# A fused sliding-window conv and ELU feed-forward layer: conv taps as the stationary operand, and one transposing transfer per super step

## The chip, the cores and the metric

The kernel runs on one core of one Trainium2 chip. The metric is the device time of one execution in microseconds (us), lower is better. Quoted times are medians of several runs. Scatter of the runs of one kernel: 0.2 to 0.4% from the lowest to the highest. The profile of an execution gives, for every instruction, its engine, start and length.

Engines are named as in the profile: PE is TensorE, PEld its weight loads, DVE is VectorE, ACT is ScalarE, POOL is GpSimd, SP is SyncE.

## The reference, cut to what matters

```python
# x: 8 x 4096 x 192 float32, weight: 8 heads x 7 taps
w = softmax(weight, axis=-1)
# causal window of 7 tokens, per head of 24 channels
out = einsum('hk,bskhg->bshg', w, windows_of(x_padded))     # "conv", 32768 tokens x 192
h = out @ w_in                                               # 192 -> 2048
g = where(h > 0, h, exp(min(h, 0)) - 1)                      # ELU
return g @ w_out                                             # 2048 -> 192, float32
```

## The kernel before

The 32768 tokens are worked off in 32 super steps of 1024 tokens (super step 0 is computed in another way at the start). A super step has 16 *pairs*. One pair is one block of 128 of the 2048 hidden columns for both halves of 512 tokens: three concurrent matmul pairs of the first product into one PSUM slot `H`, two EXPs on ACT, two clamps on POOL, and two DVE instructions that write `gT` and free the slot. PSUM is the memory that the matmuls write to. The kernel uses eight banks of it: `H` is three slots of two banks, `ops` takes two more as the accumulator of the second product. The conv of a coming super step has no bank of its own, so it takes an `H` slot too.

```python
# PE, first product of pair n: the slot must be free
k = slot_of_pair[n]
wait_slot(k)            # DVE is done with the pair that had it, or ACT with the conv
for j in range(3):
    for r in range(2):  # two row tiles, concurrent
        ins = pe.matmul(H[:, k % 3, GS * r : GS * (r + 1)],
                        w_in[HP * r : HP * (r + 1), j, FC * q : FC * (q + 1)],
                        att[HP * r : HP * (r + 1), s % 2, j, :], ...,
                        tile_position=(HP * r, 0))
# ... second product: "rounds" of two concurrent 64 x 128 x 192 matmuls from gT and w_out,
#     dealt out between the pairs; 64 rounds fill `ops` for one half (512 tokens)

# PE, conv half m: x is stationary (24 columns), the band of taps Tr is moving
for hb in range(2):
    for (w, c0, nc_, o) in PIECES[g]:
        for q in range(4):
            h = 4 * hb + q
            ins = pe.matmul(to[SLOT * q : SLOT * q + CPH, hb, o : o + nc_],
                            xg[:, s % NXB, w, CPH * h : CPH * (h + 1)],
                            Tr[:, h, CW - c0 - nc_ : CW - c0][:, ::-1],
                            start=True, stop=True, tile_position=(0, SLOT * q))

# ACT: clears the conv's slot into csb (1024 elements), and `ops` into osb once per half
a.activation(csb[:, m % 4, b0:b1, :], conv_bank(m)[:, b0:b1, :], ACT.Copy)
a.activation(osb[:, b, :, :, :].rearrange("p g k d -> p g (k d)"), ops[:, :, 0 : 2 * D], ACT.Copy)

# SP: csb goes to DRAM (`bounce`) and comes back in the layout that the first product needs
sy.dma_start(bounce[...], csb[:, m % 4, :, :])
for j in range(3):
    eng.dma_start(att[HP * g : HP * (g + 1), s % 2, j, :], src)

# DVE, pair n: ELU, and frees the slot
v.scalar_tensor_tensor(out=gT[:, s % NG3, q, u, :], in0=E[:, n % NE, u, :], scalar=1.0,
                       in1=H[:, slot_of_pair[n] % 3, GS * u : GS * (u + 1)],
                       op0=ALU.subtract, op1=ALU.max)
# ... (the start, the loads and the tail are cut)
```

## Time and profile before

| | before |
|---|---|
| time | 748.92 us (median of 4, 747.99 to 749.63) |
| span of the profiled run | 746.2 us |
| first osb evacuation | 39.01 us |
| mean half super step (8 pairs), pairs 64 to 447 | 11.341 us |

The page of the kernel before. The first line is the busy time of each engine; then come two lines of the chain that ended last (share of the span by engine, then by engine, tile and line); then groups of instructions: line, engine, operation, tiles, shapes, count, then busy us and mean ns of one, then idle time of the engine just before them.

```profile
PE 735.6 (99%) x13850; PEld 517.2 (69%) x13850; DVE 637.9 (85%) x1041; ACT 647.0 (87%) x1165; POOL 660.8 (89%) x1107
...
PE 96%; DVE 1%; ACT 1%; DMA 1%; issue 0%; POOL 0%; SPq 0%
PE ops L741 46%; PE H L706 45%; PE H L679 5%; DVE gT L561 1%; PE H L741 1%; DMA xf<-in_x_dram 1%; ACT E L499 0%; POOL E L410 0%; PE H L648 0%; PE ops L648 0%; ACT csb L479 0%; ACT xT L438 0%; PE H L616 0%; DVE xh L536 0%; SPq L755 0%
...
L561 DVE SCALAR_TENSOR_TENSOR gT<-E,H 128x512 f16<-128x512 f32 x1024 | 632.8, 682 | 92.8 <-POOL E L410 86.4
...
L741 PE MATMUL ops<-w_out,gT 64*128 64x192 f16 x8064 | 416.8, 243 | 0.3
L706 PE MATMUL H<-att,w_in 64*128 64x512 bf16 x3072 | 407.7, 377 | 2.5 <-DVE gT L561 1.9
...
L679 PE MATMUL H<-Tr,xg 128*24 128x122 bf16 (+1 forms) x2360 | 38.6, 209 | 0.0
```

PE is busy 99% and is 96% of the chain. A first-product matmul is recorded as 377 ns and a round's as 243 ns, but the next pair of matmuls starts 216 and 83 ns after the last. The records overlap by some 160 ns, so a gap of PE of up to 0.16 us doesn't show as idle time. To see it one has to subtract starts. The Trainium skill warns of this share in "Perfetto Trace Analysis", Identifying the Most-Contended Engine: matmul busy share is not a good measure of TensorE's distance from its limit. The busy share of the weight loads, one of the two measures that it names instead, is 69% here.

The timeline of PE around one conv of the kernel before (start us, length us, engine, line, operation, tiles, shapes, count):

```profile
589.14 0.82 PE L706 MATMUL H<-att,w_in 64*128 64x512 bf16 x6
589.80 0.99 PE L741 MATMUL ops<-w_out,gT 64*128 64x192 f16 x20
590.63 0.81 PE L706 MATMUL H<-att,w_in 64*128 64x512 bf16 x6
591.27 0.58 PE L741 MATMUL ops<-w_out,gT 64*128 64x192 f16 x10
591.78 0.65 PE L679 MATMUL H<-Tr,xg 128*24 128x122 bf16 x40
592.36 0.67 PE L741 MATMUL ops<-w_out,gT 64*128 64x192 f16 x12
592.87 0.81 PE L706 MATMUL H<-att,w_in 64*128 64x512 bf16 x6
```

Ten matmuls are five rounds: 591.27 + 5 x 0.083 = 591.68, but the conv (L679) starts at 591.78. That 0.10 us I take for the drain when the tiling mode changes. The conv then takes 0.58 us until the next round at 592.36. This 0.58 us holds a second drain, on the way back: in this half the last four conv matmuls, of 24 columns, start by 592.25, four such take 0.03 us, and the next round still starts only at 592.36. Over pairs 64 to 447 the way back costs 0.107 us in one half and 0.089 in the other.

From the starts of all matmuls between pairs 64 and 447 I added up what lies between them beyond the pitch of back-to-back work (0.2156 us a first-product pair of matmuls, 0.0827 us a round, 0.59 us a conv half). Before, a super step of 22.68 us has 0.20 us of drains ahead of conv and 0.33 us of gaps ahead of first products.

### The profile page before, as it was taken

Reading aid. Unit: us, or ns where it says so; the run is one execution under the profiler, and the core shown is the slowest. Engines: PE = TensorE matmul, PEld = TensorE weight load, DVE = VectorE, ACT = ScalarE, POOL = GpSimd, SP = SyncE. Lnnn points to the kernel's source line nnn. Section 1 sums busy time; section 2 is a strip of 40 time slices with the busy share of each in tenths; the row PEclk is TensorE's granted clock in tenths of the full one; section 3 lists DMA queues with packets and bytes.
Section 4 is the critical chain, followed back from the end, with each engine's and each line's share of the span. In section 5 each row is a group of like instructions: output and inputs, shape, how many; then the busy total and the mean of one; then the engine's idle time right before and its main releaser. Section 6 shows DMA issues by size and latency. Waiting matters only on the chain.

```text
span 746.2 us, 32212 instructions
## 1 busy us (share of the span) xinstructions
PE 735.6 (99%) x13850; PEld 517.2 (69%) x13850; DVE 637.9 (85%) x1041; ACT 647.0 (87%) x1165; POOL 660.8 (89%) x1107
## 2 busy tenths in 40 slices
PE   7899999999999999999999999999999999999998
PEld 4567777777777677776677777776776776777666
DVE  5988988888889889889889888888898898888894
ACT  6888888898888898888888888988888888888884
POOL 8888989989989989889989899899898898899883
PEclk9999999999999999999999999999999999999999
DMA  9654453453543543444434435535435435345112
GB/s 174 134 107 89 101 107 84 104 106 79 112 90 88 113 97 88 93 101 101 107 88 103 98 90 107 107 73 118 85 92 110 94 93 115 77 103 106 60 44 65
DMA packets 107038, 72.79 MB, mean 98 GB/s; under 512 B 44552, under 2 KB 106640, under 8 KB 106896
## 3 DMA queue, kind: packets, MB, share of 16 engines
q1 hardware_dynamic: 66384, 54.47, 24.0%
q0 software_dynamic: 40224, 15.78, 19.7%
q8 instruction: 108, 1.77, 1.0%
q10 hardware_dynamic: 288, 0.49, 0.2%
q14 instruction: 34, 0.28, 0.1%
HBM read 44.78 MB, written 41.42 MB: 116 GB/s over the span
## 4 chain that ended last, share of the span: by engine, by line
PE 96%; DVE 1%; ACT 1%; DMA 1%; issue 0%; POOL 0%; SPq 0%
PE ops L741 46%; PE H L706 45%; PE H L679 5%; DVE gT L561 1%; PE H L741 1%; DMA xf<-in_x_dram 1%; ACT E L499 0%; POOL E L410 0%; PE H L648 0%; PE ops L648 0%; ACT csb L479 0%; ACT xT L438 0%; PE H L616 0%; DVE xh L536 0%; SPq L755 0%
## 5 line engine op out<-in xcount | busy, mean ns | idle before, releaser
L561 DVE SCALAR_TENSOR_TENSOR gT<-E,H 128x512 f16<-128x512 f32 x1024 | 632.8, 682 | 92.8 <-POOL E L410 86.4
L410 POOL TENSOR_SCALAR E<-E 128x512 f32<-128x512 f32 x1024 | 604.3, 615 | 72.9 <-ACT E L499 68.0
L499 ACT ACTIVATE E<-H 128x512 f32<-128x512 f32 x1024 | 546.0, 605 | 83.3 <-PE H L706 74.6
L741 PEld LDWEIGHTS ops<-w_out,gT 64*128 64x128 f16 x8064 | 345.3, 94 | 106.6 <-ACT osb L470 10.8
L741 PE MATMUL ops<-w_out,gT 64*128 64x192 f16 x8064 | 416.8, 243 | 0.3
L706 PE MATMUL H<-att,w_in 64*128 64x512 bf16 x3072 | 407.7, 377 | 2.5 <-DVE gT L561 1.9
L706 PEld LDWEIGHTS H<-att,w_in 64*128 64x128 bf16 x3072 | 134.1, 94 | 99.2 <-issue 5.8
L479 ACT ACTIVATE csb<-H 128x1024 bf16<-128x1024 f32 x59 | 60.4, 1024 | 0.0
L470 ACT ACTIVATE osb<-ops 128x768 f32<-128x768 f32 x63 | 51.5, 817 | 6.2 <-PE ops L741 6.2
L362 POOL DMA_DIRECT2D xg<-in_x_dram x62 | 52.2, 842 | 0.4 <-issue 0.4
L679 PE MATMUL H<-Tr,xg 128*24 128x122 bf16 (+1 forms) x2360 | 38.6, 209 | 0.0
L679 PEld LDWEIGHTS H<-Tr,xg 128*24 128x24 bf16 x2360 | 29.6, 92 | 9.3 <-issue 9.3
L741 PE MATMUL H<-w_out,gT 64*128 64x192 f16 x128 | 5.9, 243 | 0.0
L572 DVE COPY osb<-H 128x192 f32<-128x192 f32 x1 | 0.4, 358 | 6.3 <-PE H L741 6.3
L741 PEld LDWEIGHTS H<-w_out,gT 64*128 64x128 f16 x128 | 5.3, 94 | 0.0
L592 PE MATMUL ops<-zw 128*128 128x512 bf16 x9 | 4.0, 631 | 1.2 <-DVE zw L511 1.2
L367 POOL DMA_DIRECT2D w_in<-in_moe_w_in_dram x7 | 4.6, 657 | 0.3 <-DMA wh<-in_weight_dram 0.3
L479 ACT ACTIVATE csb<-ops 128x512 bf16<-128x512 f32 x6 | 3.7, 623 | 0.3 <-PE ops L679 0.3
L597 PE MATMUL ops<-zw 64*128 64x512 bf16 x12 | 2.3, 380 | 1.7 <-ACT csb L479 1.7
L592 PEld LDWEIGHTS ops<-zw 128*128 128x128 bf16 x9 | 1.2, 142 | 3.2 <-issue 1.9
L679 PEld LDWEIGHTS ops<-Tr,xg 128*24 128x24 bf16 x120 | 1.6, 92 | 2.0 <-issue 2.0
L597 PEld LDWEIGHTS ops<-zw 64*128 64x128 bf16 x12 | 0.6, 94 | 3.1 <-ACT csb L479 2.7
(47 smaller groups left out, 26.1 us busy)
## 6 DMA issues: line engine op xcount, KB each, us to landing
out_dram<-osb SPq DMA_DIRECT2D x126, 192.0 KB, 2.7
conv_slots<-csb SPq DMA_DIRECT2D x62, 256.0 KB, 2.5
att<-conv_slots SPq DMA_DIRECT2D x186, 64.0 KB
xg<-in_x_dram POOLq DMA_DIRECT2D x31, 240.0 KB, 5.2
xg<-in_x_dram POOLq DMA_DIRECT2D x31, 192.0 KB, 4.5
w_out<-in_moe_w_out_dram POOLq DMA_DIRECT2D x1, 768.0 KB, 14.8
w_in<-in_moe_w_in_dram POOLq DMA_DIRECT2D x2, 240.0 KB, 8.0
xf<-in_x_dram ACTq DMA_DIRECT2D x1, 384.0 KB, 3.3
```

Source lines behind the costliest of these rows:

```text
L362: g.dma_start(xg[:, b, w0:w1, :], src).then_inc(s_x[b][part - 1], 16)
L367: g.dma_start(w_in[HP * r : HP * (r + 1), :, c0:c1], moe_w_in.rearrange("(p j) f -> p j f", j=3)[:, :, c0:c1],).then_inc(s_w[k], 16)
L410: g.tensor_scalar(out=E[:, n % NE, u, :], in0=E[:, n % NE, u, :], scalar1=1.0, scalar2=0.0, op0=ALU.min, op1=ALU.max,).then_inc(s_clp)
L470: a.activation(osb[:, b, :, :, :].rearrange("p g k d -> p g (k d)"), ops[:, :, 0 : 2 * D], ACT.Copy,).then_inc(s_oev)
L479: return a.activation(csb[:, m % 4, b0:b1, :], conv_bank(m)[:, b0:b1, :], ACT.Copy)
L499: a.activation(E[:, n % NE, u, :], H[:, k, GS * u : GS * (u + 1)], ACT.Exp).then_inc(s_exp)
L561: v.scalar_tensor_tensor(out=gT[:, s % NG3, q, u, :], in0=E[:, n % NE, u, :], scalar=1.0, in1=H[:, slot_of_pair[n] % 3, GS * u : GS * (u + ...
L592: pe.matmul(ops[:, 0, :], zw[:, 0:P], zw[:], start=True, stop=True)
L597: pe.matmul(ops[:, r, :], zw[HP * r : HP * (r + 1), 0:P], zw[HP * r : HP * (r + 1), :], start=True, stop=True, tile_position=(HP * r, 0),)
L679: ins = pe.matmul(to[SLOT * q : SLOT * q + CPH, hb, o : o + nc_], xg[:, s % NXB, w, CPH * h : CPH * (h + 1)], Tr[:, h, CW - c0 - nc_ : CW ...
L706: ins = pe.matmul(H[:, k % 3, GS * r : GS * (r + 1)], w_in[HP * r : HP * (r + 1), j, FC * q : FC * (q + 1)], att[HP * r : HP * (r + 1), s ...
L741: ins = pe.matmul(acc[:, g, d0 : d0 + D], gT[HP * rt : HP * (rt + 1), t % NG3, q, g, t0 : t0 + P], w_out[HP * rt : HP * (rt + 1), q, :], s ...
```

## The change

The intent: conv in the same tiling mode as both products, with no drain and fewer columns to stream; output already per token, so that one transposing transfer per super step replaces two writes to DRAM and six reads; a simpler load of the band. Since every conv half now takes four heads of *all* 1024 tokens, it needs both parts of x: the second part is needed half a super step sooner, and is loaded a whole one sooner. The third of the three early convs, at the start of the kernel, moves from after pair 10 to after pair 9. The core of the diff, with cuts marked by `...`:

```diff
+CW = 128
+TOK = 112
+WPG = 5
+HB = 2
+BN = HB * CPH * 2 * WPG        # 480
+GAP_SPLIT = 4
-EARLY_CONV = {3: (1, 0), 6: (1, 1), 10: (2, 0)}
+EARLY_CONV = {3: (1, 0), 6: (1, 1), 9: (2, 0)}
...
-        order.append(("c", m))
+        order.append(("c", m, 0))
+        between = []
+        if gap:
+            between, gap[:] = gap[:GAP_SPLIT], gap[GAP_SPLIT:]
+        if between:
+            order.append(("o", between))
+        order.append(("c", m, 1))
...
+        def turn_att(eng, s):
+            eng.dma_start_transpose(
+                out=att[:, s % 2, :, :].rearrange("p j (w t) -> p (j w) t", t=TOK),
+                in_=csb[0:TOK, s % 2, :],
+            ).then_inc(s_att[s % 2], 16)
...
+                    csb[:, s % 2, :].rearrange(
+                        "p (j v h i) -> p h j v i", j=3, v=2 * WPG, h=HEADS
+                    )[:, h0 : h0 + HB],
+                    conv_bank(m)[:, b, 0:BN].rearrange(
+                        "p (h v i j) -> p h j v i", h=HB, v=2 * WPG, j=3
+                    ),
...
+            v.tensor_copy(Tm[:], Tr[:, :, ::-1]).then_inc(s_tm)
...
-                    for part in range(g + 1):
-                        W(s_x[s % NXB][part], x_need[s, part])
+                        for part in range(2):
+                            W(s_x[s % NXB][part], x_need[s, part])
...
+                    for hh in range(HB):
+                        for rt in range(2):
+                            b = rt ^ turned
+                            h = 4 * u + HB * b + hh
+                            n1 = BN // HB
+                            ins = pe.matmul(
+                                to[:, b, n1 * hh : n1 * (hh + 1)],
+                                Tm[HP * rt : HP * (rt + 1), h, :],
+                                xg[HP * rt : HP * (rt + 1), s % NXB, :, :].rearrange(
+                                    "p (g w) d -> p w g d", g=2
+                                )[:, :, :, CPH * h : CPH * (h + 1)],
+                                start=(hh == 0 and not turned),
+                                stop=(hh == HB - 1 and turned == 1),
+                                tile_position=(HP * rt, 0),
+                            )
+                            if hh == HB - 1 and not turned:
+                                ins.then_inc(s_cs)
...
```

The kernel keeps the two row tiles from writing one bank at the same time, and each bank needs both, hence the two phases (`turned`), with four rounds between them.

More of the change, by code (lines that the diff above doesn't have):

```diff
@@ L19 @@
 CPH = 24
-SLOT = 32
-CW = 122
-ZW = 256
+CW = 128
[4 more added lines that the diff above has]
+GAP_SPLIT = 4
+TAP = 6
 GS = 512
@@ L25 @@
 PAD = KSIZE - 1
-NWIN = 9
 NXB = 2
@@ L41 @@
 HALO = 2
-XW = 5
-X_AT = ((3, 1), (8, 0), (11, 2))
-PIECES = (
-    ((0, 0, CW, 0), (1, 0, CW, CW), (2, 0, CW, 2 * CW), (3, 0, CW, 3 * CW), (4, 0, 24, 4 * CW)),
-    ((4, 24, 24, 0), (5, 0, CW, 24), (6, 0, CW, 24 + CW), (7, 0, CW, 24 + 2 * CW),
-     (8, 0, CW, 24 + 3 * CW)),
-)
+X_AT = ((3, 2, 1), (8, 2, 0), (11, 3, 2))
+X_LATE = (17, 3, 2)
 def bass_lightweight_conv__then__act_elu_kernel(
@@ L87, in bass_lightweight_conv__then__act_elu_kernel, with conv_at @@
     order = []
-    def conv_at(s, g):
+    def conv_at(s, g, gap=None):
         m = 2 * s + g - 2
@@ L143, in bass_lightweight_conv__then__act_elu_kernel @@
                 if at == i and s + ahead < NS:
-                    conv_at(s + ahead, g)
-        if gaps:
+                    conv_at(s + ahead, g, gaps[0] if gaps else None)
+        if gaps and gaps[0]:
             order.append(("o", gaps[0]))
@@ L181, in bass_lightweight_conv__then__act_elu_kernel @@
     place = {key: k for k, key in enumerate(finished)}
-    taps = nc.dram_tensor("conv_taps", (HEADS, ZW), BF16).ap()
-    bounce = nc.dram_tensor("conv_slots", (2, 2, P, SUP), BF16).ap()
+    taps = nc.dram_tensor("conv_taps", ((HEADS + 2) * CW,), BF16).ap()
     with ExitStack() as stack:
@@ L207, in bass_lightweight_conv__then__act_elu_kernel @@
         sel = sbuf("sel", [HEADS, P], BF16)
-        xg = sbuf("xg", [P, NXB, NWIN, D], BF16)
+        xg = sbuf("xg", [P, NXB, 2 * WPG, D], BF16)
         Tr = sbuf("Tr", [P, HEADS, CW], BF16)
-        csb = sbuf("csb", [P, 4, 2, GS], BF16)
-        att = sbuf("att", [P, 2, 3, GS], BF16)
+        Tm = sbuf("Tm", [P, HEADS, CW], BF16)
+        csb = sbuf("csb", [P, 2, 3 * 2 * WPG * HP], BF16)
+        att = sbuf("att", [P, 2, 3, WPG * TOK], BF16)
         w_in = sbuf("w_in", [P, 3, FF], BF16)
@@ L216, in bass_lightweight_conv__then__act_elu_kernel @@
         osb = sbuf("osb", [P, 2, 2, 2, D], FP32)
-        zt = sbuf("zt", [HEADS, ZW], BF16)
+        zt = sbuf("zt", [HEADS, CW], BF16)
         xf = sbuf("xf", [P, 2, QUAD, D], FP32)
@@ L230, in bass_lightweight_conv__then__act_elu_kernel @@
         s_wb = sema("s_wb")
+        s_tm = sema("s_tm")
+        s_xr = sema("s_xr")
         s_wc = sema("s_wc")
@@ L254, in bass_lightweight_conv__then__act_elu_kernel @@
         s_ce = sema("s_ce")
-        s_dw = [sema(f"s_dw{i}") for i in range(4)]
+        s_cs = sema("s_cs")
         s_band = sema("s_band")
@@ L272, in __call__ @@
                     self.eng.wait_ge(sem, value)
-        NDMA_ATT = 6
         x_need, z_need = {}, {}
@@ L322, in out_group @@
             eng.dma_start(dst, osb[:, b, g, :, :]).then_inc(s_out[b], 16)
-        def read_att(eng, W, s, g):
-            m = 2 * s + g - 2
-            W(s_dw[m % 4], 16 * (m // 4 + 1))
-            for j in range(3):
-                src = bass.AP(
-                    tensor=bounce.tensor,
-                    offset=(2 * P * (s % 2) + j) * SUP + GS * g,
-                    ap=[[SLOT * SUP, HEADS], [3 * SUP, 8], [1, GS]],
-                )
-                eng.dma_start(
-                    att[HP * g : HP * (g + 1), s % 2, j, :], src
-                ).then_inc(s_att[s % 2], 16)
+        def turn_att(eng, s):
[3 more added lines that the diff above has]
+            ).then_inc(s_att[s % 2], 16)
         @block.gpsimd
@@ L352, in load_x @@
                     W(s_cv, 2 * (s - NXB))
-                if part == 1:
-                    w0, w1, row = 0, XW, t0 - PAD
-                else:
-                    w0, w1, row = XW, NWIN, t0 + SUP - P - CW * (NWIN - 1 - XW)
+                row = t0 + GS * (part - 1) - PAD
+                v0 = WPG * (part - 1)
+                whole = WPG
+                if row + TOK * (WPG - 1) + P > NT:
+                    whole = WPG - 1
+                    rest = NT - row - TOK * whole
+                    g.dma_start(
+                        xg[0:rest, b, v0 + whole, :],
+                        x_flat[NT - rest : NT, :],
+                    ).then_inc(s_xr, 16)
                 src = bass.AP(
@@ L359, in load_x @@
                     offset=row * D,
-                    ap=[[D, P], [CW * D, w1 - w0], [1, D]],
+                    ap=[[D, P], [TOK * D, whole], [1, D]],
                 )
-                g.dma_start(xg[:, b, w0:w1, :], src).then_inc(s_x[b][part - 1], 16)
+                g.dma_start(xg[:, b, v0 : v0 + whole, :], src).then_inc(s_x[b][part - 1], 16)
             def load_w_in(k, halves):
@@ L404, in _gpsimd @@
                 s, i = divmod(n, NQ)
-                for at, part in X_AT:
-                    if at == i and s and s + NXB < NS:
-                        load_x(s + NXB, part)
+                for at, ahead, part in X_AT:
+                    if at == i and s and s + ahead < NS:
+                        load_x(s + ahead, part)
+                if n == X_LATE[0]:
+                    load_x(*X_LATE[1:])
                 for u in range(2):
@@ L441, in _scalar @@
             a.activation(
-                att[:, 0, 0, :].rearrange("p (r t) -> p r t", r=2),
+                att[:, 0, 0, 0:GS].rearrange("p (r t) -> p r t", r=2),
                 ops[:, :, 0 : GS // 2],
@@ L476, in _scalar, with conv_evac @@
             late = []
-            def conv_evac(m, b0, b1):
+            def conv_evac(m, b):
+                s, u = m // 2 + 1, m % 2
+                h0 = 4 * u + HB * b
                 return a.activation(
-                    csb[:, m % 4, b0:b1, :], conv_bank(m)[:, b0:b1, :], ACT.Copy
+                    csb[:, s % 2, :].rearrange(
[4 more added lines that the diff above has]
+                    ),
+                    ACT.Copy,
                 )
@@ L484, in _scalar @@
                 if item[0] == "c":
-                    m = item[1]
+                    _, m, turned = item
+                    if not turned:
+                        continue
                     W(s_cv, m + 1)
-                    W(s_dw[m % 4], 16 * (m // 4))
+                    s = m // 2 + 1
+                    if s > 2:
+                        W(s_att[s % 2], 16 * ((s - 1) // 2))
+                    conv_evac(m, 0)
                     if m < FREE_CONV:
-                        conv_evac(m, 0, 1)
                         late.append(m)
                     else:
-                        conv_evac(m, 0, 2).then_inc(s_ce)
+                        conv_evac(m, 1).then_inc(s_ce)
                 elif item[0] == "h":
@@ L502, in _scalar @@
                     if late:
-                        conv_evac(late.pop(), 1, 2).then_inc(s_ce)
+                        conv_evac(late.pop(), 1).then_inc(s_ce)
                 else:
@@ L528, in _vector @@
             v.tensor_scalar(
-                out=zt[:, CW - 1 : CW - 1 + KSIZE],
+                out=zt[:, TAP : TAP + KSIZE],
                 in0=whe[:],
@@ L547, in _vector @@
             v.tensor_copy(
-                att[:, 0, 1, :].rearrange("p (r t) -> p r t", r=2),
+                att[:, 0, 1, 0:GS].rearrange("p (r t) -> p r t", r=2),
                 H[:, 2, :].rearrange("p (r t) -> p r t", r=2)[:, :, 0 : GS // 2],
@@ L554, in _vector @@
             ).then_inc(s_hd)
+            W(s_band, 48)
+            v.tensor_copy(Tm[:], Tr[:, :, ::-1]).then_inc(s_tm)
             for n in range(NP):
@@ L609, in _tensor @@
             pe.matmul(
-                H[:, 2, 0:KSIZE], sel[:], zt[:, CW - 1 : CW - 1 + KSIZE], start=True, stop=True
+                H[:, 2, 0:KSIZE], sel[:], zt[:, TAP : TAP + KSIZE], start=True, stop=True
             ).then_inc(s_wb)
@@ L662, in _tensor @@
                 if item[0] == "c":
-                    m = item[1]
-                    s, g = divmod(m + 2, 2)
-                    if m == 0:
-                        W(s_band, 32)
-                    for part in range(g + 1):
-                        W(s_x[s % NXB][part], x_need[s, part])
-                    W(s_z, z_need[s])
-                    if m < FREE_CONV:
-                        conv_read(W, m - 1)
-                    else:
-                        wait_slot(slot_of_conv[m])
-                    to = conv_bank(m)
@@ L675, in _tensor @@
-                    for hb in range(2):
-                        for (w, c0, nc_, o) in PIECES[g]:
-                            for q in range(4):
-                                h = 4 * hb + q
-                                ins = pe.matmul(
-                                    to[SLOT * q : SLOT * q + CPH, hb, o : o + nc_],
-                                    xg[:, s % NXB, w, CPH * h : CPH * (h + 1)],
-                                    Tr[:, h, CW - c0 - nc_ : CW - c0][:, ::-1],
-                                    start=True,
-                                    stop=True,
-                                    tile_position=(0, SLOT * q),
-                                )
@@ L687, in _tensor @@
-                    ins.then_inc(s_cv)
+                    _, m, turned = item
+                    s, u = m // 2 + 1, m % 2
+                    if turned:
+                        W(s_cs, 2 * (m + 1))
+                    else:
+                        if m == 0:
+                            W(s_tm, 1)
+                        for part in range(2):
+                            W(s_x[s % NXB][part], x_need[s, part])
+                        if s == NS - 1:
+                            W(s_xr, 16)
+                        W(s_z, z_need[s])
+                        if m < FREE_CONV:
+                            conv_read(W, m - 1)
+                        else:
+                            wait_slot(slot_of_conv[m])
@@ L688, in _tensor @@
+                    if turned:
+                        ins.then_inc(s_cv)
                 elif item[0] == "h":
@@ L700, in _tensor @@
                         W(s_wc, 16)
-                    W(s_att[s % 2], 16 * NDMA_ATT * ((s + 1) // 2))
+                    W(s_att[s % 2], 16 * ((s + 1) // 2))
                     k = slot_of_pair[n]
@@ L708, in _tensor @@
                                 w_in[HP * r : HP * (r + 1), j, FC * q : FC * (q + 1)],
-                                att[HP * r : HP * (r + 1), s % 2, j, :],
+                                att[HP * r : HP * (r + 1), s % 2, j, 0:GS],
                                 start=(j == 0),
@@ L756, in _sync @@
             load_first(sy, 1)
+            W(s_zw, 1)
+            sy.dma_start(
+                bass.AP(tensor=taps.tensor, offset=0, ap=[[(HEADS + 1) * CW, 2], [1, CW]]),
+                zw[0:2, 0:CW],
+            ).then_inc(s_band, 16)
             W(s_wp, 1)
-            sy.dma_start(taps[:, :], zt[:, :]).then_inc(s_band, 16)
-            W(s_band, 16)
             sy.dma_start(
-                Tr[:, :, :],
-                bass.AP(tensor=taps.tensor, offset=0, ap=[[1, P], [ZW, HEADS], [1, CW]]),
+                bass.AP(tensor=taps.tensor, offset=CW, ap=[[CW, HEADS], [1, CW]]), zt[:, :]
+            ).then_inc(s_band, 16)
+            W(s_band, 32)
+            sy.dma_start(
+                Tr[:, :, :].rearrange("p h e -> p (h e)"),
+                bass.AP(tensor=taps.tensor, offset=TAP + 1, ap=[[1, P], [1, HEADS * CW]]),
             ).then_inc(s_band, 16)
@@ L769, in _sync @@
                 if item[0] == "c":
-                    m = item[1]
-                    s, g = divmod(m + 2, 2)
-                    conv_read(W, m)
-                    sy.dma_start(
-                        bounce[s % 2, :, :, GS * g : GS * (g + 1)].rearrange("b p t -> p b t"),
-                        csb[:, m % 4, :, :],
-                    ).then_inc(s_dw[m % 4], 16)
-                    if m == 1:
-                        read_att(sy, W, s, 0)
-                    if g == 1:
-                        read_att(sy, W, s, g)
-                elif item[0] == "h":
-                    s, i = divmod(item[1], NQ)
-                    if i == 1 and s >= 1 and s + 1 < NS:
-                        W(s_h, NQ * s)
-                        read_att(sy, W, s + 1, 0)
+                    _, m, turned = item
+                    s = m // 2 + 1
+                    if turned and m % 2:
+                        conv_read(W, m)
+                        W(s_h, NQ * (s - 1))
+                        turn_att(sy, s)
                 elif item[0] == "o":
```

## The prediction

> **What bounds the kernel now.** TensorE. The page's first part has PE busy 735.6 of 746.2 us (99%), and the chain that ended last is PE for 96%: second product (L741) 46%, first product (L706) 45%, conv (L679) 5%. ACT is at 87%, DVE 85%, POOL 89% and wait mostly for each other behind PE (groups view: ACT idle 74.6 us for PE).
>
> **One half super step, from the timeline at 308 to 320 us: 11.33 us.** It holds 24 first-product pairs at 0.215 us (5.17), 64 second-product rounds at 0.083 us (5.30), one conv half, and about 0.17 us of small gaps. The conv half takes 0.59 us to the next second-product matmul, and the five rounds before it take 0.52 us instead of 0.415. The Trainium skill's "TensorEngine Tiling (Array Packing)", Key Properties, says that changing the tiling mode drains TensorE; the 0.10 us agrees. So a conv half costs 0.69 us, 62 of them 43 us.
>
> **What the change does to PE.** Conv becomes eight matmuls of 240 columns in the 64x128 tiling that both products use: four pairs of 0.103 us (interpolated between 192 columns in 0.083 and 512 in 0.215) = 0.41 us, with no drain. PE alone would save 0.28 us per half, 17 us in all. I expect 0.02 to 0.08 us back where the second phase waits for the first: only four rounds (0.33 us) lie between.
>
> **Why I don't take all of it.** Every half has a second, nearly critical path: conv -> ACT evacuates conv -> EXP of the next pair -> ACT evacuates osb -> second product may start. osb ends at 312.0, PE restarts at 312.21, and the weight loads already waited 10.8 us in 62 places for osb (waits view): slack about 0.05 us. Afterwards the conv ends at about the same offset (rounds are put inside it), and two evacuations of 480 elements replace one of 1024: from 485 ns for 384 and 605 for 512, about 0.58 us each, near 1.08 us together against 1.02. PE arrives 0.28 us sooner, ACT only about 0.1 sooner, so about 0.13 us of new wait appears. Net 0.10 to 0.15 us per half: 6 to 9 us.
>
> **Transfers.** Per super step 256 KB x2 of bounce writes and six 64 KB reads become one transposing transfer of 430 KB. It has some 12 pairs (17 us) of slack: hidden. "DMA: Bandwidth & Descriptors", Latency and other measured facts, gives 261 GB/s for such a transfer.
>
> **Start.** conv needs both x parts sooner. The second part for step 2 lands at 25.7 us now, and its conv moves to about 24.2. The band's 244-byte packets go away, which should help. Net within 1 us.
>
> **Prediction:** 741 us, 8 in 10 within 731 to 749. Faster by over 2% 0.18, within 2% 0.75, slower by over 2% 0.07.
>
> **Right if:** conv's share on PE falls to about 26 us with no gap before it; ACT gains a few us; a wait of PE or of its weight loads for osb grows to 0.1 to 0.2 us per half; half a step takes 11.2 us; first-product pairs never wait for att.
>
> **Wrong if:** the evacuation, which reads PSUM with a stride of three elements and writes runs of eight, costs more per element (0.2 us each more would slow the kernel by over 1%); the moving operand in runs of 24 elements streams slower; the transposing transfer takes over 15 us; or ACT's slack is larger, and up to 17 us come through.

## The result, and the profile after

| | before | after |
|---|---|---|
| time | 748.92 us (4 runs) | 748.78 us (4 runs, 748.02 to 749.17) |
| first osb evacuation | 39.01 us | 43.35 us |
| first to last osb evacuation | 702.01 us | 697.82 us |
| mean half super step, pairs 64 to 447 | 11.341 us | 11.269 us |

The ratio is 0.9998, 95% interval 0.998 to 1.0015: the same time. A ratio here is the mean time of one kernel's fast runs over that of the other's in the same rounds, so it is not quite the ratio of the medians. The predicted 741 us was not met. The table shows at once that two things cancel: the steady state gained 4.2 us and the start lost 4.3.

The page after: busy line, chain by engine, and the groups of the conv evacuation and of the conv.

```profile
PE 731.6 (98%) x11866; PEld 505.4 (68%) x11866; DVE 638.0 (85%) x1042; ACT 646.8 (87%) x1224; POOL 664.5 (89%) x1108
...
PE 93%; DVE 2%; POOL 2%; DMA 1%; ACT 1%; issue 0%
...
L485 ACT ACTIVATE csb<-H 128x480 bf16<-128x480 f32 x118 | 60.9, 568 | 7.4 <-PE H L703 0.4
...
L703 PE MATMUL H<-xg,Tm 64*128 64x240 bf16 x472 | 44.0, 263 | 0.1
```

PE's busy share is still 98%, and ACT's total is unchanged (646.8 us against 647.0): two evacuations of 480 elements that read PSUM with a stride of three cost as much as one of 1024. The same stretch of PE after; the first line is the pair after the previous conv:

```profile
582.41 0.82 PE L735 MATMUL H<-att,w_in 64*128 64x512 bf16 x6
...
590.02 0.82 PE L735 MATMUL H<-att,w_in 64*128 64x512 bf16 x6
590.68 0.99 PE L770 MATMUL ops<-w_out,gT 64*128 64x192 f16 x20
591.50 0.81 PE L735 MATMUL H<-att,w_in 64*128 64x512 bf16 x6
592.15 0.58 PE L770 MATMUL ops<-w_out,gT 64*128 64x192 f16 x10
592.56 0.37 PE L703 MATMUL H<-xg,Tm 64*128 64x240 bf16 x4
592.82 0.50 PE L770 MATMUL ops<-w_out,gT 64*128 64x192 f16 x8
593.15 0.37 PE L703 MATMUL H<-xg,Tm 64*128 64x240 bf16 x4
593.36 0.33 PE L770 MATMUL ops<-w_out,gT 64*128 64x192 f16 x4
593.60 0.82 PE L735 MATMUL H<-att,w_in 64*128 64x512 bf16 x6
```

The drain ahead of conv is gone: five rounds from 592.15 end at 592.56, and the conv (L703) starts at 592.56. It streams in two phases of 0.205 us. But two rounds that start at 593.36 end at 593.53, and the next pair starts only at 593.60. The sums over pairs 64 to 447, per super step, worked out from the starts of all matmuls:

| per super step of two halves, us | before | after |
|---|---|---|
| conv, from its start to the next round (two halves; before, 0.20 of it is the drain on the way back) | 1.18 | 0.82 |
| drain before conv | 0.20 | 0.01 |
| gap between the first conv phase and the rounds after it | none | 0.09 |
| wait ahead of the pair after conv | 0.00 | 0.26 |
| gaps ahead of the other pairs | 0.33 | 0.34 |
| super step | 22.68 | 22.54 |

So PE's own work did fall by 0.55 us a super step, as forecast (0.28 a half); 0.40 of it are the four drains of a super step. Almost half of the 0.55 came back as a wait of PE that was not there before (what the rows leave over is in small gaps). Who is waited for? From the view of waits, before (waiter, releaser, us in total, times, longest):

```profile
PEld ops L741 <- ACT osb L470: 10.8, 62, 0.2
...
PEld H L706 <- DVE gT L561: 3.1, 3, 1.3
...
PEld ops L741 <- PE ops L741: 0.9, 3, 0.3
```

and after:

```profile
PEld H L735 <- DVE gT L579: 12.8, 42, 1.4
PEld ops L770 <- ACT osb L474: 11.4, 62, 0.2
...
PEld ops L770 <- PE ops L770: 4.6, 27, 0.3
...
PE ops L703 <- DMA xg<-in_x_dram: 3.1, 1, 3.1
```

The weight loads' wait for osb, on which the prediction rested, did not grow (11.4 against 10.8 us). What grew is the first product's wait for DVE, 12.8 us in 42 places, which is the release of a PSUM slot; and there is one wait of 3.1 us for x, at the start. A smaller wait grew too, that of a round for earlier rounds (4.6 us in 27 places against 0.9 in 3): it is the 0.09 us after the first conv phase. The rounds on the two sides of that phase write the banks in opposite order, and the later ones wait (`s_swap` in the kernel) until the earlier ones have ended; before, a conv of 0.58 us lay between them.

The issues of the transfers, before (tiles, issuing queue, kind, count, KB each, median us from issue to landing):

```profile
conv_slots<-csb SPq DMA_DIRECT2D x62, 256.0 KB, 2.5
att<-conv_slots SPq DMA_DIRECT2D x186, 64.0 KB
```

and after:

```profile
xg<-in_x_dram POOLq DMA_DIRECT2D x61, 240.0 KB, 5.6
...
att<-csb SPq DMA_TRANSPOSE x31, 6.4
```

The transposing transfer lands in 6.4 us (3.5 to 8.3). No first product waits for `att`'s transfer in the view of waits, so this part of the change neither costs nor saves time on the path. The bytes moved fell from 72.8 to 58.9 MB; no effect of that on the time is seen.

### The profile page after: what moved, and what is told of

Same layout as the page of the kernel before. It is cut to its first block, busy times and chain, and to the rows that moved or that the text cites. A ratio compares the mean times of both kernels' runs of the same rounds, so it can differ in the third digit from the quotient of the medians.

```text
span 746.5 us, 28038 instructions
## 1 busy us (share of the span) xinstructions
PE 731.6 (98%) x11866; PEld 505.4 (68%) x11866; DVE 638.0 (85%) x1042; ACT 646.8 (87%) x1224; POOL 664.5 (89%) x1108
## 4 chain that ended last, share of the span: by engine, by line
PE 93%; DVE 2%; POOL 2%; DMA 1%; ACT 1%; issue 0%
PE H L735 45%; PE ops L770 44%; PE H L703 3%; DVE gT L579 2%; DMA xg<-in_x_dram 1%; ACT E L515 1%; POOL E L414 1%; PE H L770 1%; POOL w_in L369 1%; ACT csb L485 0%; POOL xg L364 0%; PE ops L703 0%; ACT osb L474 0%; PE ops L615 0%; POOL sel L384 0%
## 5 line engine op out<-in xcount | busy, mean ns | idle before, releaser
L770 PE MATMUL ops<-w_out,gT 64*128 64x192 f16 x8064 | 426.4, 243 | 0.3
L770 PEld LDWEIGHTS ops<-w_out,gT 64*128 64x128 f16 x8064 | 346.9, 94 | 110.5 <-ACT osb L474 11.4
L735 PEld LDWEIGHTS H<-att,w_in 64*128 64x128 bf16 x3072 | 130.9, 94 | 111.7 <-DVE gT L579 12.8
L485 ACT ACTIVATE csb<-H 128x480 bf16<-128x480 f32 x118 | 60.9, 568 | 7.4 <-PE H L703 0.4
L364 POOL DMA_DIRECT2D xg<-in_x_dram x62 | 55.7, 899 | 0.1
L703 PE MATMUL H<-xg,Tm 64*128 64x240 bf16 x472 | 44.0, 263 | 0.1
L703 PEld LDWEIGHTS H<-xg,Tm 64*128 64x128 bf16 x472 | 21.2, 94 | 0.8 <-DVE gT L579 0.3
L485 ACT ACTIVATE csb<-ops 128x480 bf16<-128x480 f32 x6 | 3.5, 588 | 3.2 <-PE ops L703 3.2
L703 PE MATMUL ops<-xg,Tm 64*128 64x240 bf16 x24 | 2.7, 306 | 3.3 <-DMA xg<-in_x_dram 3.1
L703 PEld LDWEIGHTS ops<-xg,Tm 64*128 64x128 bf16 x24 | 0.9, 97 | 5.2 <-issue 3.5
## 6 DMA issues: line engine op xcount, KB each, us to landing
w_out<-in_moe_w_out_dram POOLq DMA_DIRECT2D x1, 768.0 KB, 16.1
```

The source lines that it names most:

```text
L364: g.dma_start(xg[:, b, v0 : v0 + whole, :], src).then_inc(s_x[b][part - 1], 16)
L485: return a.activation(csb[:, s % 2, :].rearrange("p (j v h i) -> p h j v i", j=3, v=2 * WPG, h=HEADS)[:, h0 : h0 + HB], conv_bank(m)[:, b, ...
L703: ins = pe.matmul(to[:, b, n1 * hh : n1 * (hh + 1)], Tm[HP * rt : HP * (rt + 1), h, :], xg[HP * rt : HP * (rt + 1), s % NXB, :, :].rearran ...
L735: ins = pe.matmul(H[:, k % 3, GS * r : GS * (r + 1)], w_in[HP * r : HP * (r + 1), j, FC * q : FC * (q + 1)], att[HP * r : HP * (r + 1), s ...
L770: ins = pe.matmul(acc[:, g, d0 : d0 + D], gT[HP * rt : HP * (rt + 1), t % NG3, q, g, t0 : t0 + P], w_out[HP * rt : HP * (rt + 1), q, :], s ...
```

## The experiments

Twelve kernels were run, each timed in three or five rounds beside the kernel before. "Half step" is always the mean over pairs 64 to 447 of its profiled run.

### Two runs at the start of the kernel

Theory: conv 0 now waits for the second x part. Before, PE at the start (timeline):

```profile
14.42 0.82 PE L706 MATMUL H<-att,w_in 64*128 64x512 bf16 x6 [0.77 <-DVE gT L561]
15.17 0.65 PE L679 MATMUL ops<-Tr,xg 128*24 128x122 bf16 x40
```

and after; in brackets stands the idle time before the row and what ended it:

```profile
14.45 0.82 PE L735 MATMUL H<-att,w_in 64*128 64x512 bf16 x6 [0.93 <-DVE gT L579]
18.33 1.23 PE L703 MATMUL ops<-xg,Tm 64*128 64x240 bf16 x8 [3.05 <-DMA xg<-in_x_dram]
```

**s_load**, the second x part of super step 1 ahead of the third piece of `w_in`:

```diff
             load_x(1, 1)
-            load_w_in(2, (0, 1))
             load_x(1, 2)
+            load_w_in(2, (0, 1))
```

> The changed kernel with the second x part of step 1 loaded before the third piece of w_in. Start theory (the 4.3 us lost before the first osb evacuation, 43.35 against 39.01 us, come from conv 0 now waiting for both x parts): conv 0 starts 2 to 3 us sooner, the first osb evacuation is at 40.5 to 42 us, time 746 to 747. Rival (the start is lost to the longer chain of the three early convs, not to x): first osb evacuation stays at about 43 us and the time at 748.8.

Measured: 748.78 us (4 runs), ratio to before 1.000 (0.998 to 1.002). The edit did what it should and did not help:

```profile
15.26 0.84 PE L703 MATMUL ops<-xg,Tm 64*128 64x240 bf16 x8
...
27.50 1.23 PE L703 MATMUL ops<-xg,Tm 64*128 64x240 bf16 x8 [3.83 <-DMA xg<-in_x_dram]
```

Conv 0 starts at 15.26 us as in the kernel before, but now conv 2 waits 3.83 us for the second x part of super step 2, and the first osb evacuation comes at 44.53 us. The expectation of 40.5 to 42 us missed. What follows: moving one load only moved the wait. The 16 transfer engines have a mean busy share of 1.03 over the first 28.5 us after and 1.05 before (packets overlap, so it can pass 1); that they are the limit of the loads is argued from this and not shown.

Two things that the traces show besides. After the long waits the granted clock of TensorE is halved for a while: 0.50 from 17.9 to 21.3 us in the changed kernel and 0.51 from 25.6 to 32.5 us in s_load, where it is 1.00 all through the start of the kernel before. Conv 2 starts at 27.48 us in the changed kernel and at 27.50 in s_load, but at the halved clock the twelve first-product matmuls after it take 2.77 us instead of 1.78, and the first osb evacuation comes 1.2 us later.

And x is not the whole of the 4.34 us. By the start of conv 2 the changed kernel is 2.34 us behind (27.48 against 25.14 us). Another 1.25 us is lost from there to the first round (4.98 us against 3.73): conv 2 now comes after pair 9, so that four pairs follow it and not three, with a wait of 0.80 us for ACT's conv evacuation among them. The last 0.75 us goes with a wait for DVE at the pair after the first conv of super step 1 (0.82 us).

**s_shift**, the loads as they were, the three early convs two pairs later:

```diff
-EARLY_CONV = {3: (1, 0), 6: (1, 1), 9: (2, 0)}
+EARLY_CONV = {5: (1, 0), 8: (1, 1), 11: (2, 0)}
```

> The changed kernel with the three early convs two pairs later (after pairs 5, 8 and 11 instead of 3, 6 and 9), loads as they were. Start theory: the pairs run while x lands, no wait of conv 0 over 0.5 us, first osb evacuation at 39 to 41 us, time about 745 to 746. Rival: first osb evacuation at 43 us or later.

Measured: 746.31 us (746.02 to 746.91), ratio 0.997 (0.9955 to 0.9985); first osb evacuation at 40.58 us; no wait of a conv for x in the view of waits; the half step is unchanged, 11.271 us. The time falls by 2.5 us against the changed kernel, as the first osb evacuation does by 2.8. The time is 0.3 us above the expected range. The start theory holds in part. Conv 2 starts at 26.22 us, 1.26 us sooner than in the changed kernel, with no wait for x. The other 1.51 us of the gain lie between conv 2 and the first osb evacuation, where two pairs follow conv 2 now and not four. The edit moved both at once, so it doesn't separate them.

### Two runs with less work on DVE

**d_dve_a** and **d_dve_b**, in the changed kernel and in the one before (wrong results):

```diff
-                        out=gT[:, s % NG3, q, u, :],
-                        in0=E[:, n % NE, u, :],
+                        out=gT[:, s % NG3, q, u, 0:w],      # w = 448 from super step 2 on (counted from 0)
+                        in0=E[:, n % NE, u, 0:w],
                         scalar=1.0,
-                        in1=H[:, slot_of_pair[n] % 3, GS * u : GS * (u + 1)],
+                        in1=H[:, slot_of_pair[n] % 3, GS * u : GS * u + w],
```

> The changed kernel with the DVE instruction of the activation cut from 512 to 448 columns from step 3 on (wrong result on purpose; about 0.07 us less of DVE in each of 1024). Slot theory (after conv the next pair waits until DVE has freed the PSUM slot of an earlier pair; the conv itself holds one of three slots): the 0.12 us wait before the pair after conv goes, a half step falls from 11.26 to about 11.1 us, time down by 6 to 10 us. Prediction's theory (PE waits for the osb evacuation on ACT): ACT is not touched, the half step stays at 11.26 us, time within 1 us of the changed kernel.

> The same cut of the DVE instruction in the kernel before (wrong result on purpose). Slot theory: PE reaches the slot just as it comes free there, so little of it shows: the half step falls by at most 0.1 us (small gaps ahead of second-product rounds that wait for gT), time down by 0 to 5 us, clearly less than in the changed kernel. Rival (DVE limits both alike): both fall by the same.

Measured: 737.06 us after (half step 11.091), 739.08 us before (half step 11.191). Against the same kernels uncut, timed in other rounds, that is 11.7 us and 9.8 us (9.1 for the second in its own rounds). The first half step is as the slot theory says, and the time fell by more than the 6 to 10 us expected; the prediction's theory, which has no DVE in it, expected nothing. The second missed: 0 to 5 us were expected. The gaps ahead of the other pairs explain it. In the kernel before they fell from 0.33 to 0.07 us a super step. Already before, pairs 7, 8, 9 and 15 of a super step start 56 to 58 ns after DVE has freed their slot. So DVE paces the middle of every half step in both kernels, not only the pair after conv. The slot theory had to be widened to a ring.

### The ring

The changed kernel at 582 to 594 us. ACT from the pair after one conv on (EXPs, osb evacuation, EXPs of the next pairs):

```profile
583.28 1.08 ACT L515 ACTIVATE E<-H 128x512 f32<-128x512 f32 x2
584.25 0.82 ACT L474 ACTIVATE osb<-ops 128x768 f32<-128x768 f32 x1
584.94 3.10 ACT L515 ACTIVATE E<-H 128x512 f32<-128x512 f32 x6
```

POOL from the second of these pairs on, and DVE:

```profile
585.64 7.12 POOL L414 TENSOR_SCALAR E<-E 128x512 f32<-128x512 f32 x12 [0.47 <-ACT E L515]
```

```profile
584.61 1.28 DVE L579 SCALAR_TENSOR_TENSOR gT<-E,H 128x512 f16<-128x512 f32 x2 [0.91 <-POOL E L414]
586.28 8.68 DVE L579 SCALAR_TENSOR_TENSOR gT<-E,H 128x512 f16<-128x512 f32 x14 [0.39 <-POOL E L414]
```

Read it as one chain, from the pair after one conv to the pair after the next. First product at 582.41 (PE timeline above), first EXP at 583.28, osb evacuation at 584.25, first EXP of the next pair at 584.94, its clamp on POOL at 585.64, its DVE instruction at 586.28, and from there DVE shows no idle time. The twelfth of these fourteen ends at 593.55 and frees the slot of the pair two back; the third slot is the conv's. The first product starts at 593.60. The steps are 0.87 + 1.66 + 0.70 + 0.64 + 7.27 + 0.05 = 11.19 us, which is that half step. (The records of DVE overlap too, by 0.08 us. From their starts, one half of a super step has a pause of 0.11 us between the eighth and the ninth of the fourteen and the other one of 0.02 us; over pairs 64 to 447 the ring takes 11.33 us in the first and 11.21 in the second. In the longer half that pause falls where the first product of pair 0 comes late, 0.146 us after its slot is free; why was not looked into.) **Neither conv, nor its evacuation, nor a second-product round is a link of it.**

In the trace, the pair after conv starts 56 to 58 ns after the recorded end of that DVE instruction in each of the 48 half steps between pairs 64 and 447. In the kernel before it starts 141 ns after it in one half and 169 ns in the other on average. So before, PE came 0.08 and 0.11 us later than the slot. That was all the room in which a faster conv could help.

### Three runs to test the ring against its rivals

**d_half_conv_a**, half of the conv matmuls left out in the changed kernel, and **d_half_conv_b**, the same in the kernel before (wrong results):

```diff
+                            if s >= 4 and hh == 0:          # changed kernel
+                                continue
...                              (`start` moves to the first matmul that is left)
-                    for hb in range(2):                     # kernel before
+                    for hb in range(2 if s < 4 else 1):
```

> The changed kernel with half of the conv matmuls left out from super step 4 on (wrong result on purpose): TensorE works 0.2 us less per half step. Ring theory (the half step is set by a ring that holds neither conv nor second-product rounds: DVE frees a PSUM slot, first product of the pair after conv, its two EXPs, the osb evacuation, the first EXP of the next pair, POOL, twelve DVE instructions, next slot; sum of traced durations about 11.28 us): half step stays at 11.25 to 11.28 us, time within 2 us of the changed kernel, and the wait before the pair after conv grows by 0.2 us. Prediction's theory (conv end, conv evacuation, EXPs, osb evacuation, PE) and plain TensorE bound: conv ends sooner, half step falls by 0.15 to 0.2 us, time down 9 to 12 us.

> The kernel before with half of the conv matmuls left out from super step 4 on (wrong result on purpose): TensorE works 0.3 us less per half step. Ring theory: only the distance down to the ring, 11.34 to about 11.27 us, is to be had: time down by 3 to 5 us. TensorE bound: half step falls by 0.3 us, time down by 15 to 18 us.

Measured: 747.28 us (half step 11.261) and 744.47 us (half step 11.254). Both are what the ring says; for a TensorE limit 9 to 12 and 15 to 18 us were expected. In the changed kernel the wait ahead of the pair after conv rose from 0.26 to 0.47 us a super step and the gap after the first conv phase from 0.09 to 0.29, together by 0.41, as much as the matmuls left out (four pairs of 0.1025 us). Where the wait shows up was expected only half right, the sum right. The first round after the first conv phase starts 0.249 us after the start of that phase, here as in the changed kernel, though the phase is half as long here: it waits for the rounds before the phase and not for conv. In the kernel before, the cut takes 0.24 us of PE work a half step (0.3 were expected) and brings the half step to 11.25 and no lower: in this kernel a faster conv is worth about 4 us and no more.

**d_evac_a**, one of the two conv evacuations left out from conv half 8 on (wrong result):

```diff
-                    conv_evac(m, 0)
+                    if m < 8:
+                        conv_evac(m, 0)
```

> The changed kernel with only the second of the two conv evacuations from conv half 8 on (wrong result on purpose): ACT works 0.5 us less per half step, straight after conv. Prediction's theory: the conv evacuation is a link of the limiting path, half step falls by 0.2 us or more, time down 8 us or more. Ring theory: the conv evacuation fits into the time in which the pair after conv still waits for its slot; half step stays within 0.05 us of 11.27, time down by less than 3 us.

Measured: 748.95 us, ratio 0.9998 (0.998 to 1.0016), half step 11.261. ACT works half a microsecond less straight after conv, and nothing happens. The prediction's chain, conv -> conv evacuation -> EXP -> osb evacuation -> PE, falls.

### Shortening a link of the ring

The osb evacuation is in the ring, and DVE idles ahead of the pair after conv (0.91 us above). **v_osb** lets DVE clear one of the two banks there:

```diff
+                banks = 1 if shared(key) else 2            # ACT
                 a.activation(
-                    osb[:, b, :, :, :].rearrange("p g k d -> p g (k d)"),
-                    ops[:, :, 0 : 2 * D],
+                    osb[:, b, 0:banks, :, :].rearrange("p g k d -> p g (k d)"),
+                    ops[:, 0:banks, 0 : 2 * D],
...
+                for key in ends_by.get(n, ()):             # DVE, ahead of pair n
+                    ...
+                    v.tensor_copy(
+                        osb[:, n_half % 2, 1, :, :].rearrange("p k d -> p (k d)"),
+                        ops[:, 1, 0 : 2 * D],
+                    ).then_inc(s_ov)
```

> The changed kernel with the osb evacuation shared: ACT takes one bank, DVE the other (384 elements each), in the time in which DVE waits ahead of the pair after conv. Correct result. Ring theory: a link of the ring gets 0.33 us shorter, of which the readiness of the next pair's first product lets about 0.15 to 0.2 through: half step 11.05 to 11.15 us, time 738 to 743. Prediction's theory: PE's start after osb comes sooner too, gain similar; plain DVE bound (all DVE work counts): half step grows by up to 0.5 us, time up by 10 us or more.

Measured: 737.60 us (736.67 to 737.78; 738 to 743 was expected), correct, ratio to before 0.9846 (0.983 to 0.986); half step 11.104 us. DVE and ACT in this run:

```profile
309.22 0.56 DVE L594 COPY osb<-ops 128x384 f32<-128x384 f32 x1 [0.43 <-PE ops L794]
309.69 1.27 DVE L602 SCALAR_TENSOR_TENSOR gT<-E,H 128x512 f16<-128x512 f32 x2
311.17 8.68 DVE L602 SCALAR_TENSOR_TENSOR gT<-E,H 128x512 f16<-128x512 f32 x14 [0.20 <-POOL E L427]
```

```profile
309.26 0.51 ACT L488 ACTIVATE osb<-ops 128x384 f32<-128x384 f32 x1
309.84 3.21 ACT L529 ACTIVATE E<-H 128x512 f32<-128x512 f32 x6
```

DVE has *more* work (0.56 us a half step) and the kernel is 11 us faster, because the work lies in a pause and the link on ACT falls from 0.69 to 0.58 us and DVE's second pause from 0.39 to 0.20. A plain limit by DVE's total is thereby out. The pair after conv still starts 57 ns after its slot is free: the ring, shorter now, is still the limit.

**b_osb**, the same edit in the kernel before, with nothing of the change:

> The kernel before with the osb evacuation shared between ACT and DVE, nothing of the change in it. Ring theory: the ring (11.27 us) gets shorter than TensorE's own half step of 11.16 to 11.19 us (work plus the two drains), so TensorE is the limit again: half step 11.17 to 11.22 us, time 739 to 742, some 3 to 5 us behind the changed kernel with the same edit if that kernel's start were equal. Rival (the change gains nothing in the steady state, ring or not): the same half step as the changed kernel with this edit, 11.10 us.

Measured: 742.08 us (6 runs, 740.46 to 743.05), ratio 0.9914; half step 11.221, both just above the expected ranges. Here the drains (0.20 us a super step ahead of conv, as much again behind it) are among the largest gaps left, and nothing waits ahead of the pair after conv, which starts 209 and 153 ns after its slot is free. So once the ring is out of the way, the change is worth 11.221 - 11.104 = 0.117 us a half step, some 7 us over 62, of which its slower start takes back about 3.

### Three runs for a version that beats both

**v_osb_shift** is v_osb with the later convs of s_shift.

> The changed kernel with both edits: osb evacuation shared, and the three early convs two pairs later. If start and ring are separate causes, their gains add: about 2.5 us at the start and 11 us from the ring, time 734 to 736, first osb evacuation at about 40.5 us, half step 11.10 us. If the later convs only move a wait into the first steps, the time stays at 737 to 738.

Measured: 737.36 us, half step 11.106 us: no gain over v_osb beyond the scatter. PE at the start:

```profile
18.09 0.83 PE L726 MATMUL ops<-xg,Tm 64*128 64x240 bf16 x8 [0.41 <-DMA xg<-in_x_dram]
...
26.03 1.45 PE L758 MATMUL H<-att,w_in 64*128 64x512 bf16 x6 [2.46 <-DMA w_in<-w_in]
```

The conv hardly waits for x any more, but pair 10 waits 2.46 us for the last piece of `w_in`. That piece is a copy from one half of `w_in` to the other (`w_in<-w_in`), which SP issues once its source has landed; the source, loaded behind the second x part, landed at 19.71 us and the copy at 25.99. The granted clock was 0.50 for the 3.4 us after this wait as well. The expected 734 to 736 us missed, as in s_load because a wait only moved.

**v_start** is v_osb with early convs after pairs 7, 9 and 11, the fourth piece of `w_in` ahead of the second x part, and `w_out` last. **v_start2** has the same loads and the convs after pairs 6, 8 and 11.

```diff
             load_x(1, 1)
             load_w_in(2, (0, 1))
-            load_x(1, 2)
             load_w_in(3, (0,))
+            load_x(1, 2)
             load_x(2, 1)
+            load_x(2, 2)
             ... w_out ...
-            load_x(2, 2)
```

> The changed kernel with the shared osb evacuation, the early convs after pairs 7, 9 and 11, and the start's loads in another order: the fourth piece of w_in ahead of the second x part of step 1, w_out last. Start theory (the start is one saturated transfer queue; conv 0 and pair 10 each wait for a transfer, and order and place decide who waits): the wait of pair 10 for the copied w_in (2.46 us in the last run) falls under 0.7 us, conv 0 waits under 0.5 us, first second-product round at 29.5 to 31 us, first osb evacuation at 40 to 41.5 us, time 734.5 to 736. If one of the two waits only moves to the other transfer: 737 or more.

> As the run above with the early convs after pairs 6, 8 and 11. Start theory: conv 0 reaches its x part about 1 us before it lands and waits for it, so 0.3 to 1 us slower than the run above; equal if the extra wait is hidden behind the wait for the copied w_in.

Measured: v_start 736.74 us (735.58 to 737.67), v_start2 736.27 us (735.24 to 736.76), ratio 0.9835 (0.982 to 0.985). Neither kernel has a PE wait for x of any size; first osb evacuation at 41.78 and 40.39 us. The time of v_start missed its range by 0.7 us (and its first osb evacuation by 0.3), and v_start2 was to be slower than it or equal but came out 0.5 us faster. The two differ by less than the scatter of their runs. v_start2 is the fastest kernel, correct, 1.65% below the kernel before.

## Why the prediction was wrong, point by point

- **"PE alone would save 0.28 us per half"**: right. Conv with its way back fell from 0.59 to 0.41 us a half and the drain of 0.10 us ahead of it went. Half of that first saving was the drain on the way back, which I had counted as conv. 0.045 us came back ("0.02 to 0.08" forecast), but by luck: not the second phase waited for the first, the rounds after the first phase waited for the rounds before it.
- **"Every half has a second, nearly critical path: conv -> ACT evacuates conv -> EXP of the next pair -> ACT evacuates osb -> second product may start"**: this is the step that failed. There is a second limit, and I had its size right (0.13 us of new wait a half, forecast and measured) for the wrong reason, which is luck. d_evac_a took half of the first link away and nothing changed; the weight loads' wait for osb stayed at 11 us. What the runs showed in its place is the ring through DVE's slot release, in which conv has no part. I looked for a rival path only at the engine where the work moved, ACT, and took DVE's 85% as slack. But DVE ran fourteen instructions with no idle time shown in every half step already before, and slots were taken 57 ns after their release at pairs 7, 8, 9 and 15; both were in the trace.
- **"Net 0.10 to 0.15 us per half: 6 to 9 us"**: 0.072 us per half, 4.2 us between the first and the last osb evacuation. The room down to the ring was 0.08 to 0.11 us, and d_half_conv_b confirms that about 4 us is all there was.
- **"Start ... Net within 1 us"**: the other failure, mis-sized as a term: it cost 4.3 us, more than half of the miss. I had seen that the second x part of super step 2 lands at 25.6 us and its conv comes at about 24, and did not ask the same of conv 0. In the kernel before, the second part of super step 1 lands at 16.1 us and conv 0 runs at 15.2; after, it landed at 18.2. "The band's 244-byte packets go away, which should help" was not borne out: x landed later, not sooner. I did not isolate why; one thing that grew is every second x load, from 192 to 240 KB. Nor had I priced the third early conv's move from pair 10 to pair 9: 1.25 of the 4.3 us were lost between conv 2 and the first round.
- **"Transfers ... hidden"**: right, with no PE wait for `att`'s transfer.
- **"ACT gains a few us"**: wrong, it stayed equal.

What stays open: how much of the lost start each of the two edits there (x needed sooner, conv 2 moved) costs alone; a wait of 0.8 us for DVE at the pair after the first conv of super step 1, in all versions of the changed kernel; why x lands two microseconds later in the start.

## What to carry to other kernels

A TensorE at 99% busy can still wait: subtract the starts of its matmuls before you call it the limit, and check how long after its release each buffer is taken. Here a constant 57 ns, in every half step, marked the ring that sets the pace; time saved on work outside that ring was worth only the distance down to it. Shorten a link of the ring, even by giving more work to the busiest engine in a pause, and price a change that needs its inputs sooner at the start of the kernel: here the second x part landed two microseconds later than before.

## What the Trainium skill lacked or had wrong

- "TensorEngine Tiling (Array Packing)", Key Properties, says that a change of tiling mode drains TensorE but gives no figure. Here PE lost 0.109 and 0.092 us ahead of the two conv halves, and 0.107 and 0.089 us on the way back.
- "DMA: Bandwidth & Descriptors", Latency and other measured facts, gives 261 GB/s for a transposing transfer (measured on one kernel, with a non-contiguous middle dimension). This one, 112 x 1920 elements of two bytes (430 KB) from SBUF to SBUF beside other traffic, took 6.4 us from issue to landing (median of 31; 3.5 at best), 67 GB/s (122 at best), latency included, so the two figures are not quite alike, and its issue held SP for 1.6 us. I found no speed there for such a transfer beside other traffic.
- "TensorE: Matmul & The Clock Gate", Wait — 56ns, not 53.3ns?, says that start to start never drops below about 25 ns. The forty conv matmuls on four column tiles start 11.7 ns apart on average (four within some 15 ns, the next four about 53 ns after the first): across tiles that floor doesn't hold, and this section doesn't say that it is meant for one tile.
- No page that I found gives a figure for a strided PSUM read on ACT, or for a moving operand in runs of 24 elements. Reading every third element, 480 of them took 568 ns, in line with 485 ns for 384 contiguous ones (a copy) and 605 for 512 (the EXPs). The moving operand in runs of 24 streamed at full pace: a pair of 240 columns took 0.1025 us, between 0.083 for 192 and 0.216 for 512.
- No page that I found has the hand-off of a PSUM slot: 57 ns from the recorded end of the DVE instruction to the first matmul that overwrites the slot, where PE was already waiting.
